# Two gated spectral filters on one core: halves of x added and subtracted in bf16 before the first matmuls, in place of a fold after them

## The chip, the cores and the metric

The kernel runs on one core of a Trainium2 chip. The core has a matrix engine (PE, with its weight loads shown apart as PEld), a vector engine (DVE), a scalar engine (ACT), a general engine (POOL, called GpSimd in code) and a queue engine (SP) that issues nearly all DMA transfers here. Each engine works through its own instruction list strictly in order; an instruction that waits holds up everything behind it in the same list. The metric is the device time of one execution in microseconds (us), lower is better.

## The reference, cut to what matters

For an input x of 2048 rows and 1024 columns, two spectral filters A and B, and a gate vector:

```
g = sigmoid(sum over columns of x * gate_w)           # one number per row
a = irfft2(rfft2(x) * (A_w_r + i A_w_i))              # 2048 x 1024
b = irfft2(rfft2(x) * (B_w_r + i B_w_i))
out = g * a + (1 - g) * b                             # bf16
```

Both filters work on the same x, so the forward transform is made once, the two weighted products and the two inverse transforms share the work, and the row gate is put into the last transform over rows.

## The kernel before, in words

Row index s is split as s = 16*s2 + s1, with s2 (128 values) on the partitions. The columns are brought in by the host as four quarters of 256, the second and fourth reversed, so that symmetric and antisymmetric combinations over the columns are plain sums and differences of quarters. Even output frequencies (parity 0) and odd ones (parity 1) of the column transform are computed separately. Everything runs in three stretches that overlap:

1. **First transform (F1).** For each of 16 s1 values, `f1` (L321) multiplies x by a 128x128 table over s2. For each parity it makes eight matmuls of 128 columns: halves of x are added or subtracted inside PSUM accumulation (second pass with F or -F), which gives two 256-wide parts per parity. The two parts have then to be added and subtracted (the *fold*) to make the two 256-wide inputs of the next step. Two routes exist: `FC` copies one part from PSUM to scratch in `wx` and `FD` folds on DVE (two `tensor_tensor`, one operand from PSUM); `FX` copies both parts and `FP` folds on POOL. The result lies in `y`.
2. **Sixteen units n (0 to 7 parity 0, 8 to 15 parity 1).** For each unit: `F2` (column transform, L450, two half tiles), `T` (copy PSUM to SBUF), `F3` (L480, twiddle and 16-point transform), `X` (copy to SBUF), `P` (L494, product with the weights of both filters, two instructions of 128x2048 for the real and imaginary r), for n below 8 also `Y`, `NA`, `N` (a patch of one column), `J` (`i1`, L537, inverse 16-point transform, two PSUM tiles of 1024), `R` (copy of each tile to SBUF as `rl`), `H` (256 KB stored to a DRAM scratch). The copies are on ACT or DVE as the order list says. Weights W:0 to W:7 land in `Ro`, W:8 to W:11 in `wx`, W:12 to W:15 in `y`.
3. **Second transform and output.** When all eight units of a parity are stored, `L` (L554) loads the scratch back transposed, 512 KB for each pair v of s1 values, into `Re` (parity 0) or `Ro` (parity 1). `V` (`i2`, L565) applies the inverse transform over rows with the gate in its weights `EA` and `EB`; `VC` copies to SBUF; `C` or `U` (L590, L581) applies the inverse column transform: `C` gives two 256-wide parts that still have to be mixed, `U` gives the finished sums at twice the PE columns. Even results end as f32 in `Re` (`E`, or `EX` on ACT or DVE and `EQ` on POOL); the odd ones are added to and subtracted from them (`OR` on DVE straight from PSUM, `OC`+`OP` on POOL, `QD`+`QP` for the two-part form), and `S` stores rows of the output.

The gate: `GH`, `GC`, `GT`, `GK`, `GZ` compute it during stretch 2, `GS` (L434) is the sigmoid on ACT, and `GW` (L439, L440) multiplies it into `EA` and `EB`, four s1 values at a time, on DVE. `tab` (L297) runs a sigmoid on a scratch tile early, so that ACT's table load stands at the start.

What sets the order of the work is `ORDER` (L24 to L68), a list written out: the kernel goes through its tokens one by one, and each appends its instructions to the lists of its engines, under manual scheduling. A token such as `T:3:1:A` reads: copy half 1 of unit 3 on ACT; the last numbers of PE tokens name PSUM banks. So an engine's list is the list's tokens for that engine in the order written, and SP's list holds x, constants, weights, `H`, `L` and `S` in that order too. The `rl` tile has five buffers (`RLB`), `p` three (`PB`).

In the list before, `warm:8 c:A:F1 c:A:gws tab:A` come first (eight matmuls on a zeroed tile, the memset for them on DVE; two constants on ACT's queue; the table). The last units end so: `J:14` and `J:15`, then `H:14:0`, `H:15:1`, `H:15:0`, and behind them on SP `L:0:6`, `L:0:7` and all `L:1`. On PE four `V` and two `C` of parity 0 stand before `J:15`, the other twelve `V` and fourteen `C` between it and the first `V` of parity 1, `V:1:0`.

## Time and profile before

| | |
|---|---|
| runs shown | 117.52, 116.9, 117.24 us; median 117.24 |
| profiled execution | span 115.6 us from the first to the last instruction, granted PE clock 0.985 |
| own time of the profiled execution | not given apart from the span; the median of the runs is 1.64 us above the span |
| PE | 103.6 us busy (90%), 1619 matmuls |
| DVE | 97.0 us (84%), 164 instructions |
| ACT | 84.4 us (73%), 138 instructions |
| POOL | 46.2 us (40%), 74 instructions |
| DMA | 36.79 MB, mean 318 GB/s |

The page gives the span in 40 slices (2.89 us each) with the busy share of each engine in tenths, the chain of work that ended last, and groups of instructions with their mean duration. A matmul's recorded duration contains its pipeline latency, so a busy PE is not PE at its peak: eight 256-column matmuls in a row take 0.109 us each from start to start, while the record of one is 0.273 us. Rates in the text are therefore taken from starts.

### The profile page before, as it was taken

Reading aid. Unit: us, or ns where it says so; the run is one execution under the profiler, and the core shown is the slowest. Engines: PE = TensorE matmul, PEld = TensorE weight load, DVE = VectorE, ACT = ScalarE, POOL = GpSimd, SP = SyncE. Lnnn points to the kernel's source line nnn. Section 1 sums busy time; section 2 is a strip of 40 time slices with the busy share of each in tenths; the row PEclk is TensorE's granted clock in tenths of the full one; section 3 lists DMA queues with packets and bytes.
Section 4 is the critical chain, followed back from the end, with each engine's and each line's share of the span. In section 5 each row is a group of like instructions: output and inputs, shape, how many; then the busy total and the mean of one; then the engine's idle time right before and its main releaser. Section 6 shows DMA issues by size and latency. Waiting matters only on the chain.

```text
span 115.6 us, 3953 instructions
## 1 busy us (share of the span) xinstructions
PE 103.6 (90%) x1619; PEld 71.3 (62%) x1619; DVE 97.0 (84%) x164; ACT 84.4 (73%) x138; POOL 46.2 (40%) x74
## 2 busy tenths in 40 slices
PE   5999999999999699898889899989979999999900
PEld 2499989875567256463445357459859765867400
DVE  0099999999999999999899999999157349999970
ACT  4009488999999999999999999977735844534300
POOL 1066995900000000000000000057986999999920
PEclk9999999999999999999999999999999999999995
DMA  3999999999579999669999999999999992482874
GB/s 90 348 326 401 403 374 367 363 397 408 210 222 324 371 394 373 169 263 397 350 293 354 348 306 401 254 357 382 352 353 411 403 418 98 198 346 119 327 279 181
DMA packets 17794, 36.79 MB, mean 318 GB/s; under 512 B 1904, under 2 KB 10736, under 8 KB 17776
## 3 DMA queue, kind: packets, MB, share of 16 engines
q1 hardware_dynamic: 17488, 36.44, 87.5%
q8 instruction: 12, 0.20, 0.6%
q10 hardware_dynamic: 288, 0.10, 0.4%
q14 instruction: 6, 0.05, 0.1%
HBM read 23.96 MB, written 12.58 MB: 316 GB/s over the span
## 4 chain that ended last, share of the span: by engine, by line
PE 39%; DVE 19%; DMA 16%; ACT 16%; issue 4%; SPq 1%; DVEq 1%; ACTq 0%
ACT rl L204 11%; PE ps L581 9%; PE ps L565 8%; DVE y L382 7%; PE ps L450 6%; PE ps L334 5%; DMA sc<-rl 5%; DMA re<-sc 4%; DMA ig<-cst_ig 4%; PE ps L537 3%; DMA re<-in_x_dram 3%; PE ps L480 3%; DVE p L494 3%; ACT X L204 3%; PE ps L590 3%
## 5 line engine op out<-in xcount | busy, mean ns | idle before, releaser
L615 POOL TENSOR_TENSOR re<-wx 128x256 f32<-128x256 f32 x28 | 19.6, 730 | 55.3 <-DMA re<-sc 53.1
L204 ACT CAST rl<-ps 128x1024 bf16<-128x1024 f32 x29 | 29.6, 1142 | 0.7 <-ACT wx L204 0.7
L204 ACT COPY wx<-ps 128x256 f32<-128x256 f32 (+1 forms) x39 | 17.2, 498 | 10.5 <-PE ps L334 8.2
L537 PE MATMUL ps<-p,wj 32*64 32x512 bf16 x512 | 20.5, 381 | 2.5 <-ACT rl L204 2.0
L204 ACT CAST V<-ps 128x512 bf16<-128x512 f32 x25 | 13.8, 601 | 11.3 <-PE ps L565 8.4
L494 DVE TENSOR_TENSOR p<-X,ro 128x2048 bf16<-128x2048 bf16 x16 | 19.1, 1215 | 0.0
L450 PE MATMUL ps<-fd,y 128*128 128x256 bf16 x128 | 16.5, 273 | 0.4 <-ACT rl L204 0.4
L382 DVE TENSOR_TENSOR y<-ps,wx 128x256 bf16<-128x256 f32 x48 | 16.4, 412 | 0.1
L334 PEld LDWEIGHTS <-re 128*128 128x128 bf16 x256 | 15.2, 100 | 1.6 <-DMA re<-in_x_dram 1.0
L334 PE MATMUL ps<-f,re 128*128 128x128 bf16 x256 | 15.8, 224 | 0.3
L204 ACT CAST T<-ps 128x512 bf16<-128x512 f32 x26 | 15.5, 693 | 0.0
L537 PEld LDWEIGHTS <-wj 32*64 32x64 bf16 x512 | 8.4, 103 | 10.6 <-issue 7.5
L382 POOL TENSOR_TENSOR y<-wx 128x256 bf16<-128x256 f32 x16 | 11.1, 734 | 8.2 <-DVE wx L206 5.9
L635 DVE TENSOR_TENSOR ot<-re,ps 128x512 bf16<-128x512 f32 x22 | 13.8, 681 | 0.4
L450 PEld LDWEIGHTS <-y 128*128 128x128 bf16 x128 | 11.5, 97 | 4.1 <-issue 2.6
L581 PE MATMUL ps<-ig,V 128*128 128x512 bf16 x56 | 13.4, 380 | 0.0
L204 ACT CAST X<-ps 128x1024 bf16<-128x1024 f32 x12 | 13.2, 1118 | 0.0
L206 DVE COPY wx<-ps 128x512 f32<-128x512 f32 (+1 forms) x10 | 5.8, 578 | 7.4 <-PE ps L334 4.8
L480 PE MATMUL ps<-T,wf 64*64 64x256 bf16 (+1 forms) x128 | 10.2, 332 | 1.1 <-DVE np L514 1.0
L590 PE MATMUL ps<-ig,V 128*128 128x256 bf16 x72 | 9.7, 273 | 0.0
L494 DVE TENSOR_TENSOR p<-X,wx 128x2048 bf16<-128x2048 bf16 x8 | 9.4, 1217 | 0.0
L494 DVE TENSOR_TENSOR p<-X,y 128x2048 bf16<-128x2048 bf16 x8 | 9.3, 1215 | 0.0
(60 smaller groups left out, 138.4 us busy)
## 6 DMA issues: line engine op xcount, KB each, us to landing
sc<-rl SPq DMA_DIRECT2D x32, 256.0 KB, 4.7
ro<-in_we_dram SPq DMA_DIRECT2D x8, 512.0 KB, 8.3
re<-sc SPq DMA_DIRECT2D x8, 512.0 KB, 6.1
ro<-sc SPq DMA_DIRECT2D x8, 512.0 KB, 7.7
re<-in_x_dram SPq DMA_DIRECT2D x7, 512.0 KB, 8.0
out_dram<-ot SPq DMA_DIRECT2D x7, 512.0 KB, 2.6
wx<-in_wo_dram SPq DMA_DIRECT2D x4, 512.0 KB, 6.6
y<-in_wo_dram SPq DMA_DIRECT2D x4, 512.0 KB, 5.0
```

What stands on the lines that cost most here:

```text
L204: nc.scalar.copy(out=out, in_=in_)
L334: nc.tensor.matmul(o, lhsT=lh, rhs=rh, start=(h == 0), stop=(h == 1))
L382: Q[e].tensor_tensor(yo[:, v, k:k + n, s1, :], a.rearrange("p (k c) -> p k c", c=4), b.rearrange("p (k c) -> p k c", c=4), op)
L450: nc.tensor.matmul(ps[:, v * 256:v * 256 + 256], lhsT=y[:, v, par, b, 2 * t:2 * t + 2, :, :].rearrange("p j s c -> p (j s c)"), rhs=C["FD" ...
L480: nc.tensor.matmul(view(ps[ho, tt * 512:(tt + 1) * 512], dst), lhsT=lh, rhs=view(T[hp(jh), tt, :], src), start=(w == 0), stop=(w == 1))
L494: nc.vector.tensor_tensor(p[:, r], xb, w, ALU.mult)
L537: nc.tensor.matmul(o, lhsT=lh, rhs=src[r, ri, wi, tt], start=(q == 0), stop=(q == 3))
L565: nc.tensor.matmul(ps[:, ch * 128:ch * 128 + 128], lhsT=RR[par][:, v, ch // 2, s, c0 + 256 * ab:c0 + 256 * ab + 128], rhs=Ew[:, s1, :], st ...
L581: nc.tensor.matmul(ps, lhsT=Vs[par, v][:, s, ch, :], rhs=rh, start=(ch == 0), stop=(ch == 3))
L590: nc.tensor.matmul(ps[:, o:o + 256], lhsT=Vs[par, v][:, s, ch, :], rhs=g[:, o:o + 256], start=(ch % 2 == 0), stop=(ch % 2 == 1))
L615: Q[e].tensor_tensor(EV[:, v, s, 256 * h:256 * h + 256], t[:, 0], t[:, 1], (ALU.add, ALU.subtract)[h])
L635: nc.vector.tensor_tensor(otile(v)[:, s, h, :], EV[:, v, s], PS["O", 1, v, s], (ALU.add, ALU.subtract)[h])
```

## The change

What it does:

- **F1.** A new function `presum` (`PF`) runs on DVE as x arrives: u = lower half + upper half of the columns into `wx`, and the difference in place over the lower half of x, both bf16 in SBUF. It is called once for one s1 twice and then for two s1 at a time. `f1` then makes, for each parity, four matmuls of 256 columns whose table operand is [F, F] or [F, -F], so the fold over the quarters happens in PSUM accumulation. `FE` (`f1e`) copies the finished 512 or 1024 columns to `y`, on ACT or DVE. `FC`, `FD`, `FX` and `FP` are gone, and with them all POOL work of this stretch. `y` is laid out with parity outermost.
- **Products.** `P:n:b` makes both r in one instruction of 128x4096. Weights W:12 to W:15 land in `Ro`, in the places of W:0 to W:3, instead of `y`.
- **Gate weights.** `GW` for s1 0 to 3 and 12 to 15 is on POOL; the other two stay on DVE. `neg` (the negated table for `F3`) is on POOL instead of ACT.
- **Order list.** It is another list from end to end. In front: x:0, x:1, the F1 table on ACT's queue, x:2, `PF:0:1`, and only then `warm:8`, so the memset for the warm matmuls stands on DVE behind the two instructions of `PF:0`. `tab:A` stands close to the end; ACT's list then holds two table loads, one at its start and one in front of the first `GS`. The units run in the order 0, 1, 2, 3, 7, 4, 5, 8, 6, 9, 12, 13, 10, 11, 15, 14. Nine `V` and six `C` of parity 0 stand before `J:14` on PE, and seven `V` and nine `C` between it and the first `V` of parity 1, which is `V:1:5`. All `L:0` stand on SP with eight stores (of units 10 to 15) still behind the last of them; `L:1:5` is the first transfer behind `H:14:1`, the last store. The last stretch has twenty `C` and twelve `U` (before: eighteen and fourteen), 24 `EQ` (28), eight `QD` (four) and eighteen `OR` (22). The mixed rows `QP` are on DVE five times and on POOL three times (before: POOL four times). `EX` copies go to `y` instead of `wx`.

The core of the diff:

```
 ORDER = """
-warm:8 c:A:F1 c:A:gws tab:A x:S:0:1 x:S:1:1 x:S:2:2 x:S:4:2 x:S:6:2 x:S:8:2 x:S:10:2 x:S:12:2 x:S:14:2 c:S:FD:0:1
-F1:1:o:0 F1:1:e:1 FX:1:o:D F1:0:o:2 FC:1:e:D F1:0:e:3 FP:1:o FD:1:e F1:3:o:0 F1:2:e:4 FC:0:e:D F1:3:e:1 gc:P FD:0:e
...
+x:S:0:1 x:S:1:1 c:A:F1 x:S:2:2 PF:0:1 warm:8 PF:1:1 F1:1:0 F1:0:2 x:S:4:2 x:S:6:2 x:S:8:2 x:S:10:2 x:S:12:2 PF:2:2
+F1:3:4 FE:0:A x:S:14:2 c:S:EZ c:S:gws gc:P c:S:w0 PF:4:2 F1:2:6 FE:1:A FE:2:A F1:4:2 F1:5:0 FE:4:A c:S:WJ:0:4
...
-    def f1(s, par, k):
+    def presum(s, n):
+
+        s, n = int(s), int(n)
+        lo, hi = x[:, s:s + n, 0:512], x[:, s:s + n, 512:1024]
+        nc.vector.tensor_tensor(uw[:, s:s + n, :], lo, hi, ALU.add)
+        nc.vector.tensor_tensor(lo, lo, hi, ALU.subtract)
+
+    def f1(s, k, h=""):
+
         s1 = int(s)
...
+        for e in (0, 1) if h == "" else (int(h),):
+            ps = PS["F1", s1, e] = ptile(int(k) + (e if h == "" else 0))
             for b in range(2):
...
+                for pr in range(2):
+                    c = pr * 256 + b * 128
+                    lh = x[:, s1, c:c + 128] if e else uw[:, s1, c:c + 128]
+                    rh = F1[:, 0:2] if pr else bc(F1[:, 0, :]).to_broadcast([P, 2, 128])
+                    o = ps.rearrange("p (v b k) -> p v b k", v=2, b=2)[:, :, b]
+                    nc.tensor.matmul(o, lhsT=lh, rhs=rh, start=(pr == 0), stop=(pr == 1))
+        if h == "":
+            PS["F1", s1] = ptile(k, 2)
+
+    def f1e(s, e, h=""):
 
         s1 = int(s)
...
+        r = slice(0, 256) if h == "" else slice(128 * int(h), 128 * int(h) + 128)
+        src = PS["F1", s1] if h == "" else PS["F1", s1, int(h)]
+        cp(e, yo[:, r, s1, :], src.rearrange("p (k c) -> p k c", c=4))
...
     def prod(n, r):
-        n, r = int(n), int(r)
-        if r == 0:
+        n = int(n)
+        if n not in Ps:
             Ps[n] = wk.tile([P, 2, 2, 4, 256], BF16, name="p", tag="p", bufs=PB)
         X, w, p = Xs[n], Ws[n], Ps[n]
...
+        if r == "b":
+            xb = X[:].rearrange("p r t (a m) -> p r t a m", a=1).to_broadcast([P, 2, 2, 4, 256])
+            wb = w.rearrange("p (r t) a m -> p r t a m", r=1).to_broadcast([P, 2, 2, 4, 256])
+            nc.vector.tensor_tensor(p[:], xb, wb, ALU.mult)
```

## The prediction

> **What bounds the kernel now.** I read the page's slices first, then the engines' instructions in order of time, then the chain that ended last. The slices:
>
> ```profile
> span 115.6 us, 3953 instructions
> ...
> PE   5999999999999699898889899989979999999900
> ...
> DVE  0099999999999999999899999999157349999970
> ACT  4009488999999999999999999977735844534300
> POOL 1066995900000000000000000057986999999920
> ```
>
> Between slices 7 and 26 (20 to 78 us) both DVE and ACT are at nine tenths: the sixteen units are bound by these two together, not by PE. From 80 us ACT and DVE have gaps and PE has none. At the end DVE is full again. The instructions in order of time give the rates (start to start) and the joints:
>
> ```profile
> 1.17 3.60 PE L248 MATMUL ps<-ea 128*128 128x512 bf16 x8 [1.17 <-DVE ea L245]
> 4.87 14.91 PE L334 MATMUL ps<-f,re 128*128 128x128 bf16 x240
> ...
> 24.53 2.35 DVE L494 TENSOR_TENSOR p<-X,ro 128x2048 bf16<-128x2048 bf16 x2
> 71.08 4.62 DVE L494 TENSOR_TENSOR p<-X,y 128x2048 bf16<-128x2048 bf16 x4
> 75.61 0.68 DVE L206 COPY wx<-ps 128x512 f32<-128x512 f32 x1
> 103.12 8.93 DVE L635 TENSOR_TENSOR ot<-re,ps 128x512 bf16<-128x512 f32 x14
> ...
> 47.31 2.97 ACT L204 CAST rl<-ps 128x1024 bf16<-128x1024 f32 x3
> 50.02 1.18 ACT L204 CAST X<-ps 128x1024 bf16<-128x1024 f32 x1
> 77.10 1.01 ACT L204 CAST rl<-ps 128x1024 bf16<-128x1024 f32 x1 [0.71 <-ACT wx L204]
> ...
> 75.96 1.06 PE L537 MATMUL ps<-p,wj 32*64 32x512 bf16 x28 [0.31 <-ACT rl L204]
> 72.74 7.60 SPq L549 DMA_DIRECT2D sc<-rl  x9
> 83.95 4.47 SPq L554 DMA_DIRECT2D ro<-sc  x8
> 89.06 0.99 PEld L565 LDWEIGHTS <-ro 128*128 128x128 bf16 x16
> ```
>
> The reader is to see four joints. F1 starts on PE at 4.87, the first product at 24.53, the last product ends at 75.61 and the last `J` at 77.02. The last store is issued by 80.34, the first `L:1` at 83.95 (SP waits for the stores), the first `V` of parity 1 runs at 89.06. DVE ends at 112.05 and the span 3.55 us later. In the chain of waits
>
> ```profile
> 79.96 0.39 SPq L549
> 80.35 0.05 issue
> 80.40 5.18 DMA re<-sc
> 85.58 0.05 issue
> 85.62 0.62 PE ps L565 x8
> ```
>
> the last store's issue leads to a load, and the load to PE, which then stands without a gap to 108.28. From the last `J` to `V:1:0` PE had 12 `V` (0.45 us each) and 14 `C` (0.44) to do, 11.5 us, so it covered the trip through DRAM but for 0.8 us at 85.6.
>
> Rates: on ACT `T` 0.48, `X` 0.91, `rl` 0.90; on DVE a 512-wide PSUM copy 0.60, a 1024-wide one 1.13, `P` 1.13 (four in 4.53), `OR` 0.64. PE's 256-column matmul 0.109, 128-column 0.058.
>
> **Start and F1.** The warm matmuls run at 0.43 us each, twice the 0.215 us that `U`'s 512 columns take later, and they stand first on PE. Their memset now stands behind `PF:0`, which waits for x:0. Issue at 0.72 plus the shortest landing of these loads, 3.0, gives 3.7. `PF:0` is two two-input SBUF instructions of 512, 0.45 + 0.42 by the `GW` rows (L439, L440), the memset 0.27, the warm block 3.6: PE comes to F1 at 8.5, not 4.87. F1 itself is 128 x 0.109 = 14.0 us instead of 256 x 0.058 = 14.8, and DVE's `presum` (4 x 0.42 + 14 x 0.69, 11 us) follows x as it lands and ends near 17, so it is hidden. `FE` on ACT can start at 8.5 + 1.74 = 10.3; eight of 1024 at 0.95 (between `X`, 0.91, and twice the gate copy with the same short runs, 0.51) and seven of 512 at 0.50 stand before the first `T`: 11.1 us, plus small waits, so 22.0 against 20.45 before. The first product: `F3` waits for the second `T` at 23.0, 0.55 on PE, `X` 0.91: 24.9 against 24.53. The 3.6 us late start thus costs only 0.4 at the first product, because the fold's 16.4 us on DVE and 11.1 on POOL (groups of L382) are gone. Four half `F1` with their copies (1.5 us ACT, 0.6 DVE) are still to come, where before nothing was left.
>
> **The units.** `P` of 4096: 512 elements take 0.424, 2048 take 1.215, so 0.515 ns an element and 0.16 fixed, 2.27 alone, 2.19 in a row; two of 2048 are 2.26. Sixteen save 1.1 us. The other bound is the pace of a one-per-cycle cast (1024 in 1.22), 4.4 each, 35 us more; I take 2.19, since the instruction of before has the same kind of repeated operand. Two pairs of `GW` leave DVE (1.6), `neg` leaves ACT (0.75); ACT gets a table load (1.28, the row at the start).
>
> The page "ScalarE: Activation LUTs" (What ACT_TABLE_LOAD costs) adds a drain of about 1.38 us to the load, which would make this 2.66 and the total 1.4 more; no row here shows the drain.
>
> DVE from the first to the last product: 35.0 + patches 2.4 + eight `T` 4.8 + `FE` 0.6 + `X` 1.13 + five `rl` 5.65 + `GW` 0.8 + 0.1 = 50.5, so 75.4 at no gap (before: 51.1). ACT from its first `T` to the copy `R:14:0` of the last unit: 22 `T` 10.6, 15 `X` 13.6, 25 `rl` 22.5, three `FE` 1.5, gate copy and sigmoids 2.3, table 1.3, nine `VC` and five `EX` that the list puts among them 6.7: 58.5, so 80.5 at no gap. Before, the same count from 25.0 to the end of `R:15:1` (78.11) gives 51.3 in 53.1: 97%. Two full lists that hand work to each other lose that much, so I take 97% again: 82.3. `P:14` waits for `X:14` and then ends at 77.8 (75.4 if DVE alone decided), `J:14` also for `R:15:0` (1.13), which frees its bank, and ends near 80.
>
> **The trip through DRAM.** Behind `R:14:0`: issue of the store 0.4, 3.6 until the first `L:1` (80.34 to 83.95), 4.8 to landing (the shortest of these loads): `V:1:5` at 82.3 + 8.8 = 91.1. PE has seven `V` and nine `C` for that time, 7.1 us, so it is free by 87 and stands some 4 us. This is the step that costs: before, 11.5 us of work lay there. Ends: 80.5 + 0.4 + 2.4 (the shorter store in the chain, 70.30 to 72.64) + 4.8 = 88.1, and 91.1.
>
> **The last stretch.** From `V:1:5`, PE has 16 `V`, 5 `C` and 12 `U` (0.86): 19.7 us (before 20.1 from `V:1:0`). DVE's first `QD` can start after a `V`, a copy and two `C`, 1.8, and it has 8 `QD` (0.62), 5 `QP` (0.6 by the PSUM copies of that size; 0.68 the recorded one) and 18 `OR`: 19.5, so 21.3 at no gap; its last two `OR` need the last `U` at 19.7 plus the waits at its start. I take 22.0, before 23.0 (89.06 to 112.05). POOL has 27 us of `EQ`, `OP`, `QP` (before 32) and no longer decides.
>
> `QP` and two `GW` pairs bring something the trace hardly shows: DVE with two SBUF operands while POOL reads SBUF. One row: POOL's `EQ` at 79.17 starts while DVE's L440 (78.92, 0.42) runs, and takes 0.77 instead of 0.72; L440 is not longer. I take nothing. The other end is one POOL instruction of 0.73 to 1.29 waited for by each of five `QP` and by three products and `GW`, 6 to 10 us; below nothing is excluded, since no engine is sped up by it.
>
> The page "SBUF — State Buffer" (Who interferes with whom) states that such a pair locks the other out for the whole instruction. The row above overlapped by 0.17 us, which speaks against a full lock; by the page I would add half a POOL instruction to each of some eight meetings, about 4 us, an estimate.
>
> **Sum.** 91.1 + 22.0 + 3.55 = 116.65 against 115.6: 1.05 more. The profiled span lies 1.64 below the median of the runs, which I take as what lies around it: 118.3.
>
> **Rivals.**
> - *The trip is covered, faster.* If ACT and DVE keep their lists without gaps and the store lands in 2.4, `V:1:5` is at 88.1 and the time 88.1 + 22.0 + 3.55 + 1.64 = 115.3; with the longer store 116.5. For it: DVE idles only 0.4 us in 24.5 to 75.6. Against: ACT's 97%. It decides when `R:14:0` ends before 81. I put it at 115.9.
> - *POOL and DVE block each other.* Half of the 6 us above, in the stretch where DVE decides: 118.3 + 3 = 121.3. For it: `QP` stands on DVE among 27 us of POOL work. Against: the row at 79.17.
> - *It evens out.* The units are worth what they were, the exchange is 1 us better than taken: 117.2.
> - *The 4096 product loses its pace:* 150 us and more; under 2 in 100, outside the range.
>
> **How the numbers follow.** Forecast (118.3, own range 116.9 to 120) 0.38; covered trip 0.36; blocking 0.12; evens out 0.14. About 0.5% (0.6 us) is what a measurement of this kernel can tell from no change. Faster: the 0.36 and 0.02 of the third; slower: 0.34 of the forecast and the 0.12; same: the rest, 0.04 + 0.12. The range runs from 114.2 (the covered trip with 1 us more in the units, less than a tenth below) to 121.3 (a tenth above).
>
> **What would show it.** Right: F1 on PE near 8.5; first product near 25; DVE and ACT full to about 78 and 82; PE without work for 3 to 5 us right before `V:1:5` at 90 to 92; DVE ending 22 us later; products of 2.27; `GW` on POOL 1.3 each. Wrong: PE busy through that joint, or F1 near 5; products over 3 us; DVE's `QP` well over 0.7 (then the blocking rival). What would overturn the sum is a different efficiency of the two full lists: 3% of 58 us is 1.8 us, more than the whole difference forecast.

## The result, and the profile after

The changed kernel takes 124.25 us (median of 4 runs, 123.63 to 125.33) against 117.24 of the kernel before: the ratio is 1.062, with an interval of 1.054 to 1.069. Slower was right; the size was not: 118.3 us was forecast, with a range up to 121.3. The profiled execution took 125.33 us, the longest of the four, so its segments add up to about 1 us more than the median. Times, ratios and intervals of all versions below leave out runs more than 1.5% above the fastest run of the same version.

The page of the changed kernel: its span, and the span in 40 slices of 3.08 us with busy shares in tenths.

```profile
span 123.2 us, 3610 instructions
...
PE   0399999999999998988698977599992999949900
DVE  0569944799998999899589999975882499999960
ACT  4004999899999998999999959859581863454300
POOL 1000059400000000000607706185989847853980
```

No engine has much more work than before in total (PE 3.0 us less, POOL 0.3, DVE 1.5 and ACT 4.3 more), yet the span is 7.6 us longer: most of the time went into standing. PE is thin at the start, at 58 us (slice 20), from 71 to 80 (slices 24 to 26), at 92 (slice 31), at 108 (slice 36) and at the end.

To say where, each span is cut at five events that every version has: the first product on DVE, the end of the last unit's `J` on PE, the first issue of an `L:1` on SP, the first `V` of parity 1 on PE, and DVE's end. "Predicted" is the sum of the prediction cut at the same events.

| us | to first product | units (to end of last J) | to first L:1 | to first V of parity 1 | last stretch (to DVE's end) | to end of span | span |
|---|---|---|---|---|---|---|---|
| before | 24.5 | 52.5 | 6.9 | 5.1 | 23.0 | 3.55 | 115.6 |
| predicted | 24.9 | 55.1 | 6.3 | 4.8 | 22.0 | 3.55 | 116.65 |
| after | 25.1 | 60.5 | 5.8 | 3.75 | 23.8 | 4.3 | 123.2 |

The last `J`, the first `L:1` and the first `V` of parity 1 after:

```profile
84.51 1.07 PE L499 MATMUL ps<-p,wj 32*64 32x512 bf16 x32
...
91.38 4.00 SPq L516 DMA_DIRECT2D ro<-sc  x8
...
95.13 0.23 PE L527 MATMUL ps<-ea,ro 128*128 128x128 bf16 x1 [2.39 <-DMA ro<-sc]
```

Each version was profiled once, so it matters how far these segments vary by themselves. Four versions have the same list as the changed kernel up to the last `J` (the changed kernel, all `QP` on POOL, and two of the versions of the last stretch): their units take 60.5, 59.4, 60.6 and 61.9 us, the last with PE's clock halved for 3.41 us of them (last section). The first product of the eight versions with this start and no other change before it comes at 24.5 to 26.05. A difference of 1 us in one of these two segments of one trace is therefore not told from no difference.

Against the prediction the profiled execution is 6.55 us longer: +5.4 in the units, +1.8 in the last stretch, +0.7 at the end, +0.2 at the start, and -1.5 in the trip through DRAM.

### The profile page after: what moved, and what is told of

Same layout as the page of the kernel before. It is cut to its first block, busy times and chain, and to the rows that moved or that the text cites. A ratio compares the mean times of both kernels' runs of the same rounds, so it can differ in the third digit from the quotient of the medians.

```text
span 123.2 us, 3610 instructions
## 1 busy us (share of the span) xinstructions
PE 100.6 (82%) x1489; PEld 67.2 (54%) x1491; DVE 98.5 (80%) x119; ACT 88.7 (72%) x129; POOL 46.5 (38%) x59
## 4 chain that ended last, share of the span: by engine, by line
PE 38%; ACT 20%; DVE 16%; DMA 14%; issue 6%; POOL 2%; POOLq 1%; SPq 1%; DVEq 0%; ACTq 0%
ACT y L200 8%; PE ps L527 6%; PE ps L404 6%; DMA re<-sc 5%; PE ps L499 5%; PE ps L437 5%; ACT rl L200 5%; DVE p L453 4%; PE ps L543 4%; PE ps L337 3%; DMA sc<-rl 3%; DMA ro<-sc 3%; DVE ot L607 3%; PE ps L245 3%; DVE rl L202 3%
## 5 line engine op out<-in xcount | busy, mean ns | idle before, releaser
L453 DVE TENSOR_TENSOR p<-X,ro 128x4096 bf16<-128x4096 bf16 x12 | 27.9, 2328 | 0.0
L575 POOL TENSOR_TENSOR re<-y 128x256 f32<-128x256 f32 x24 | 20.2, 870 | 9.5 <-ACT y L200 9.0
L200 ACT CAST y<-ps 128x512 bf16<-128x512 f32 (+1 forms) x18 | 12.6, 808 | 8.4 <-PE ps L337 8.4
L437 PE MATMUL ps<-T,wf 64*64 64x512 bf16 (+1 forms) x128 | 10.6, 333 | 2.0 <-DVE T L202 1.0
L202 DVE CAST rl<-ps 128x1024 bf16<-128x1024 f32 x7 | 8.5, 1220 | 4.1 <-ACT rl L200 1.4
L453 DVE TENSOR_TENSOR p<-X,wx 128x4096 bf16<-128x4096 bf16 x4 | 10.1, 2525 | 0.0
L322 DVE TENSOR_TENSOR wx<-re 128x1024 bf16<-128x1024 bf16 (+1 forms) x9 | 5.6, 623 | 5.4 <-DMA re<-in_x_dram 5.4
L527 PE MATMUL ps<-ea,ro 128*128 128x128 bf16 x64 | 7.9, 219 | 2.4 <-DMA ro<-sc 2.4
L527 PEld LDWEIGHTS <-re 128*128 128x128 bf16 x128 | 7.6, 98 | 3.7 <-DMA re<-sc 1.9
L527 PE MATMUL ps<-ea,re 128*128 128x128 bf16 x64 | 8.3, 220 | 1.6 <-DMA re<-sc 1.6
```

Of the source, the lines that this page charges most:

```text
L200: nc.scalar.copy(out=out, in_=in_)
L202: Q[e].tensor_copy(out=out, in_=in_)
L322: nc.vector.tensor_tensor(uw[:, s:s + n, :], lo, hi, ALU.add)
L437: nc.tensor.matmul(view(ps[ho, tt * 512:(tt + 1) * 512], dst), lhsT=lh, rhs=view(T[hp(jh), tt, :], src), start=(w == 0), stop=(w == 1))
L453: nc.vector.tensor_tensor(p[:], xb, wb, ALU.mult)
L527: nc.tensor.matmul(ps[:, ch * 128:ch * 128 + 128], lhsT=RR[par][:, v, ch // 2, s, c0 + 256 * ab:c0 + 256 * ab + 128], rhs=Ew[:, s1, :], st ...
```

## What the profile of the changed kernel shows, place by place

**DVE and POOL shut each other out.** The timeline of DVE, then that of POOL, in the second half of the units (start, duration, engine, line, operation, output and input, count, idle time before and its releaser):

```profile
65.90 3.24 DVE L453 TENSOR_TENSOR p<-X,wx 128x4096 bf16<-128x4096 bf16 x1
69.06 1.37 DVE L391 TENSOR_TENSOR ea<-ea,e 128x512 bf16<-128x512 bf16 x1
...
73.14 2.28 DVE L453 TENSOR_TENSOR p<-X,wx 128x4096 bf16<-128x4096 bf16 x1
75.34 2.82 DVE L453 TENSOR_TENSOR p<-X,ro 128x4096 bf16<-128x4096 bf16 x1
```

```profile
59.42 1.15 POOL L391 TENSOR_TENSOR ea<-ea,e 128x512 bf16<-128x512 bf16 x1 [36.45 <-ACT ea L386]
...
65.47 1.52 POOL L391 TENSOR_TENSOR ea<-ea,e 128x512 bf16<-128x512 bf16 x1 [3.67 <-ACT ea L386]
67.07 3.08 POOL L392 TENSOR_TENSOR eb<-e,ea 128x512 bf16<-128x512 bf16 x1
73.79 2.22 POOL L575 TENSOR_TENSOR re<-y 128x256 f32<-128x256 f32 x1 [3.63 <-ACT y L200]
```

A product is 2.28 us alone, `GW` on POOL 1.15 (row at 59.42), `EQ` 0.73 alone. The product that starts at 65.90 is recorded at 3.24, because POOL's `GW` has the memory until some 66.9 (65.47 + 1.52, less the 0.1 us by which records overlap); POOL's next instruction, issued at 67.07, then ends only at 70.15, 1.0 after the product is through (its record is 3.08). The `GW` half at 69.06 on DVE takes 1.37 instead of 0.42. At 73.79 the same happens with `EQ`: 2.22 instead of 0.73, and it makes the product at 75.34 wait in turn: 2.82. DVE loses 0.96 + 0.95 + 0.54 = 2.45 us in this stretch, and from 62.43 to the end of the last product (81.49) it is never idle for more than 0.04 us, so the last product is late by all of it.

**A load stands behind a store, and PE behind the load.** SP's queue, and the PE instruction that waits:

```profile
72.65 0.37 SPq L511 DMA_DIRECT2D sc<-rl  x1
73.07 1.88 SPq L516 DMA_DIRECT2D re<-sc  x2
```

```profile
80.19 0.23 PE L527 MATMUL ps<-ea,re 128*128 128x128 bf16 x1 [1.62 <-DMA re<-sc]
81.19 1.07 PE L499 MATMUL ps<-p,wj 32*64 32x512 bf16 x32
```

The second of the two loads issued from 73.07 on is `L:0:1` (issued at 73.58, landed at 80.15). It stands on SP behind `L:0:2` and `H:13:0`, the store at 72.65, which waits for a copy that DVE finishes at 72.63; of that copy's lateness, 0.96 + 0.95 us are the two meetings before it. `V:0:1` on PE waits for that load until 80.19, and behind it in PE's list stands `J:15` (81.19), whose product was done at 78.16. The last `J` follows at 84.51, 3.0 us after its own product, so in this trace it is PE's list that sets it; the first `L:1` issues at 91.38 and `V:1:5` runs at 95.13.

**The last stretch.** DVE, then POOL:

```profile
97.19 2.48 DVE L602 TENSOR_TENSOR pq<-re,ps 128x512 f32<-128x512 f32 x4 [4.00 <-PE ps L552]
...
102.41 3.50 DVE L607 TENSOR_TENSOR ot<-pq 128x512 bf16<-128x512 f32 x3
...
107.62 2.36 DVE L607 TENSOR_TENSOR ot<-pq 128x512 bf16<-128x512 f32 x2
109.90 9.05 DVE L595 TENSOR_TENSOR ot<-re,ps 128x512 bf16<-128x512 f32 x15
```

```profile
104.22 1.13 POOL L575 TENSOR_TENSOR re<-y 128x256 f32<-128x256 f32 x1
105.31 1.72 POOL L607 TENSOR_TENSOR ot<-pq 128x512 bf16<-128x512 f32 x1
...
112.84 2.50 POOL L591 TENSOR_TENSOR ot<-re,wx 128x512 bf16<-128x512 f32 x2 [3.42 <-DMA out_dram<-ot]
```

From 97.19 to 118.95 DVE is never idle for more than 0.22 us. Five `QP` (L607) take 5.86 us, 1.17 each, where the prediction put 0.6; POOL's instructions beside them grow too (1.72 for `QP`, 1.13 for `EQ`; 1.27 and 0.73 alone). POOL then stands 3.42 us for an output buffer, because the first store on SP is that of v = 5, which waits for DVE's last `QP` and issues at 110.05 (before: 98.51). So POOL ends at 119.71, after DVE, and the last store with it: 4.3 instead of 3.55 behind DVE's end. The stores on SP, before and after:

```profile
98.51 13.90 SPq L652 DMA_DIRECT2D out_dram<-ot  x9
```

```profile
110.05 10.02 SPq L612 DMA_DIRECT2D out_dram<-ot  x9
```

## The experiments

Diffs name tokens of the order list; all start from the changed kernel unless said otherwise.

**GW back on DVE.**

```
-... GW:P:0 ... GW:P:12 ...
+... GW:D:0 ... GW:D:12 ...
```

> The changed kernel with both GpSimd gate-weight pairs back on DVE (nothing else). Exclusion theory (a DVE instruction with two SBUF operands and a POOL instruction wait for each other to the end): the product of 3.24 us at 65.90 and the DVE gate weight of 1.37 us at 69.06 go back to 2.28 and 0.42, the POOL pair of 1.52 and 3.08 is gone; DVE gains 1.9 of waits and pays 4 x 0.40 = 1.6, so the time moves by -1 to +0.5 us from 124.25. Rival (GpSimd is free help, the long rows are something else): DVE only pays, +1.6 us, and a product over 3 us stays.

123.62 and 125.41 us, 1.061 [1.051, 1.072]. No gain, as the theory of an exclusive lock had it: what DVE no longer waits (1.9) it now works (1.7). The rows say the same: the product and the `GW` pair in the places of the long rows above are back at their own lengths, which the rival excluded.

```profile
66.69 2.28 DVE L452 TENSOR_TENSOR p<-X,wx 128x4096 bf16<-128x4096 bf16 x1
68.89 0.42 DVE L390 TENSOR_TENSOR ea<-ea,e 128x512 bf16<-128x512 bf16 x1
69.35 0.42 DVE L391 TENSOR_TENSOR eb<-e,ea 128x512 bf16<-128x512 bf16 x1
```

The units take 61.7 us in the trace, but PE's clock is 0.50 in them from 81.29 to 84.70, while PE works off its list before the last `J`; the version with that half clock and `GW` on POOL has 61.9. So the trace shows neither gain nor loss of the edit in the units.

**The loads up.** `L:0:1`, `L:0:7` and `L:0:2` right behind `L:0:6`.

```
-L:0:6 H:12:1 L:0:4 ... L:0:3 L:0:7 ... H:13:0 ... L:0:2 ... L:0:1 ...
+L:0:6 L:0:1 L:0:7 L:0:2 H:12:1 L:0:4 ... L:0:3 ... H:13:0 ...
```

> The changed kernel with the loads L:0:1, L:0:7 and L:0:2 right behind L:0:6 on SP, in front of the stores of units 12 and 13. Queue theory (V:0:1 waits until 80.19 for a load that stands behind a store on SP, and J:15 stands behind V:0:1 on PE): V:0:1 no longer waits, J:15 starts by 78.5 instead of 81.26, the last J ends 2 to 3 us sooner, time -2 to -3 us, 121.5 to 122. Rival (the two full lists of DVE and ACT set the last J anyway): the wait moves to the next item, time within 0.6 us of 124.25.

123.13 and 123.94 us. PE's wait at 80 is gone, the units take 58.4 us (-2.1; in the other versions that have the load in its old place that wait is 1.0 to 2.1 us) and the first `L:1` issues at 88.64. The end moved by 1.1 only: the last stretch became 25.4 us. The reason is in the windows of PE at its standstill (us; busy us of PE, PEld, DVE, ACT, POOL with counts; then the granted clock, DMA share, GB/s):

```profile
90.21:93.62 3.41, 1.20 (x20) 1.11 (x20) 0.52 (x1) 0.69 (x2) 3.41 (x6) 1.00 0.94 375
93.62:97.03 3.41, 3.41 (x25) 2.77 (x23) 1.70 (x3) 1.83 (x5) 1.95 (x3) 0.50 1.03 420
97.03:100.44 3.41, 3.41 (x55) 3.32 (x54) 2.48 (x5) 2.18 (x5) 1.27 (x1) 1.00 1.02 407
```

PE stood 2.21 us for the first `L:1`, and the granted clock then was 0.50 for 3.41 us: 1.7 us of PE's work lost, against 1.55 us by which the stretch is longer than in the changed kernel's profile, where the clock stayed at 1.00.

**All QP on POOL.**

```
-QP:3:0:1:D QP:5:1:1:D QP:3:1:1:D ... QP:5:0:0:D QP:5:0:1:D
+QP:3:0:1:P QP:5:1:1:P QP:3:1:1:P ... QP:5:0:0:P QP:5:0:1:P
```

> The changed kernel with all eight QP on POOL instead of three. Exclusion theory: DVE loses five instructions of 1.14 (5.7 us) from its last stretch, POOL gains five but its own go from 1.7 to 1.8 back to 1.28; DVE ends 3 to 5 us sooner, POOL then ends last, time -1.5 to -3 us. Rival (POOL was already the last engine, at 119.7, so more work there lengthens it): +1 to +3 us.

124.81 and 125.82 us, 1.068 [1.060, 1.076]. The theory's gain of 1.5 to 3 us is not there; the middle, 1.1 us more than the changed kernel, is at the low end of what the rival said, and the interval overlaps the changed kernel's. In the trace POOL becomes what the stores wait for (first one at 111.93), and DVE stands 6.0 us for PE; but that execution took 127.69 us and has PE's clock at 0.50 for two times 3.41 us in the last stretch, so how much of it is POOL's is not shown.

**Warm matmuls and table load in front.**

```
-x:S:0:1 x:S:1:1 c:A:F1 x:S:2:2 PF:0:1 warm:8 PF:1:1 ... V:1:0:1:6 tab:A U:1:2:1:3
+warm:8 x:S:0:1 x:S:1:1 c:A:F1 tab:A x:S:2:2 PF:0:1 PF:1:1 ... V:1:0:1:6 U:1:2:1:3
```

> The changed kernel with the warm matmuls first in the list and the table token right behind the F1 table, as in the kernel before. F1 on PE starts at 5.0 to 5.8 instead of 8.73, ACT's list loses 1.28 us at 57. Theory that ACT and DVE carry the start through the units: the first product comes 2 to 3 us sooner, the table another 1.3, time -3 to -4.5 us, 120 to 121. Rival (the late start is hidden, as the prediction had it, and only the table counts): -0.5 to -1.5 us.

121.6 and 122.39 us, 1.040 [1.033, 1.047]. `F1` starts at 4.96 instead of 8.5, the first product at 22.8: 1.7 us earlier than in the kernel before. The first `L:1` issues 4.2 us earlier, the span is 2.7 shorter; the granted clock behind PE's 2.44 us standstill was 0.50 for 3.41 us here too, and the last stretch took 25.4. The two edits were not tried apart; in the changed kernel PE stood 1.28 us for the activation behind the table load at 57, and here it does not.

**GW and loads together.** Both diffs above.

> The changed kernel with two edits together: both GW pairs back from POOL to DVE (alone they changed nothing), and L:0:1, L:0:7, L:0:2 right behind L:0:6 on SP (alone the first L:1 issued 2.7 us earlier). Theory 'two causes, one behind the other': while V:0:1 holds PE until 80 the DVE locks lie hidden, and the other way round; together the first L:1 issues 3.5 to 5 us earlier than the changed kernel's 91.4, so at 86.4 to 87.9, and the last product ends at 78 to 79.5. Rival 'the two full lists simply lose more than 3%': the first L:1 stays where the loads alone put it, at 88 to 89, and the last product ends near 81. For the end both say little: with the last stretch bound by its own order (first store near 109), 122.5 to 124.5 us by either.

122.42 us (122.07 to 122.43), 1.040 [1.036, 1.044]. As the events stand, the first `L:1` (89.53) and the end of the last product (81.19) are near the rival's figures (88 to 89, near 81), not the theory's 3.5 to 5 us. But the profiled execution took 124.65 us and has its first product only at 26.05; counted from there the units take 57.4 us, 1.0 less than with the loads alone. That is within what two traces of one list differ by, so for the locks' price on the path it shows no more than "about 1 us or nothing"; the times, about 1 us below those with the loads alone, point to the former. The last stretch has the clock at 0.50 for 3.41 us too and takes 25.2.

**The last stretch without QP, two versions.**

```
-C:1:5:1:0 QD:5:1:1 ... QP:5:1:0:P ... C:1:3:1:4 QD:3:1:1 ... S:S:5 ... S:S:3
+U:1:5:1:0 OR:5:1:1 ... U:1:3:1:4 OR:3:1:1 ...
-E:5:1:A E:5:0:D ... E:3:1:A E:3:0:A
+EX:5:1:y:A EQ:5:1:0:P EQ:5:1:1:P EX:5:0:y:D ... EX:3:0:y:A EQ:3:0:0:P EQ:3:0:1:P
```

> The changed kernel with the odd rows of v = 5 and v = 3 made as the others are: U in place of C (four times), OR in place of QD (eight), no QP, the even parts through EX and EQ on POOL, and each store right behind its last OR. Theory 'the last stretch is DVE's list, made longer by QP at 1.17 instead of 0.6': from V:1:5 DVE has 26 OR of 0.61, so 15.9 us instead of 21.8, and PE (19.7 and four times 0.4) decides with about 21.5; the first output store issues near 101 to 103 instead of 110.05, POOL's 3.4 us wait on the stores is gone, and the span ends 2 to 3 us earlier: 121.3 to 122.5 us. Rival 'POOL is the bound of this stretch': eight more EQ (5.8) against three QP (4.8) delay the EQ that OR waits for, DVE stands waiting for POOL, and the time stays at 124 us or above. Rival 'the output's 4 MB set the end': first store earlier, end the same.

> The changed kernel with the warm matmuls and the table load at the front, the three loads L:0:1, L:0:7, L:0:2 up, and v = 5 and 3 in the last stretch as in e6_tail. Theory 'three separate losses, start, joint and last stretch, that add once the last stretch follows': 4 us at the first L:1 from the start, 1.5 to 2.7 more from the loads, 2 to 3 from the last stretch: first L:1 at 84.5 to 86.5, 116 to 119 us. Rival 'they overlap, and something further stands behind': 119.5 to 121.5 us, with DVE or PE idle for over 3 us in the last stretch.

132.35 us (1.127 [1.122, 1.132]) and 125.75 (1.069 [1.066, 1.072]): both misses. In both, the copies of v = 5 and 3 go into slots whose content had still to be added, so some even rows are sums of other data; the instructions are those described. What spoilt the test is my own edit: with the stores right behind the last `OR` of v = 5 and 3, SP holds later `L:1` behind them (the fourth load issues at 102.08 in the first version), and the seventeen `EQ` that POOL has from 94.6 to 107.0 hold DVE for 4.13 us. They say only that loads must not stand behind stores here, and that POOL's list is near full.

**v = 5 alone, and its store behind the last load.**

```
-E:5:1:A EQ:4:1:1:P E:5:0:D ... C:1:5:1:0 QD:5:1:1 ... QP:5:1:0:P ... S:S:5 (after the last QP)
+EX:5:1:w:A EQ:4:1:1:P EX:5:0:w:D EQ:5:1:0:P EQ:5:1:1:P EQ:5:0:0:P EQ:5:0:1:P ... U:1:5:1:0 OR:5:1:1 ... L:1:0 S:S:5
```

> The changed kernel with the odd rows of v = 5 alone made as most others are: U in place of C, four OR in place of four QD and four QP, the even parts through EX into the space of W:8 to W:11 and four EQ on POOL ahead of those that stand there; the store of v = 5 behind the last load on SP. Theory 'QP beside POOL at 1.17 makes the last stretch DVE's': DVE has 3.5 us less to do, first output store at 102 to 106 instead of 110, the span 1.5 to 2.5 us shorter: 121.5 to 123 us. Rival 'POOL is the next bound': OR waits for the EQ of v = 5 or 2, DVE stands over 2 us in the last stretch, 123.8 us or more.

124.81 us (124.46 to 125.28), 1.060 [1.053, 1.068]: no gain. The time is the rival's, but not for its reason. The first store went to 102.80, POOL's wait for a buffer is gone and the end is 3.58 behind DVE again. But the stretch took 24.0 us: the clock was 0.50 from 95.99 to 99.40, right behind PE's 2.37 us standstill, DVE stood 6.0 us before its first `OR`, and from 95.9 to 117.4 the chain of work that ended last runs on PE alone, matmul behind matmul. With PE's clock at 1.00 the same stretch takes 22.4 us (everything together, below).

**The price of QP and of a meeting.** Instructions on scratch data: `ZQ` has QP's form (on DVE), `ZP` EQ's (on POOL).

```
+P:3:b ZQ ZQ ... P:4:b ZQ ZP ZP ZP ZP ZQ ZQ ZQ ...
...
+        nc.vector.tensor_tensor(zb(512).rearrange("p (s d) -> p s d", s=2), t[:, :, 0], t[:, :, 1], ALU.add)
...
+        nc.gpsimd.tensor_tensor(zb(1408).bitcast(F32), zb(512).bitcast(F32), zv()[:, 0, 0], ALU.add)
```

> The changed kernel with instructions of QP's form (two f32 operands of 128x512 from SBUF, bf16 out) added on DVE on a scratch tile, two where POOL does nothing (behind the product of unit 3) and four beside four added f32 additions of 128x256 on POOL (behind the product of unit 4). Price 'QP costs 1.1 us by itself, because of its operands': the first two take 1.1 to 1.2 each, as long as the recorded 1.14 to 1.17. Price 'QP costs 0.6 to 0.7 and the rest is POOL's lock': the first two 0.6 to 0.7, those beside POOL 1.1 to 1.4. In both the four beside POOL show what the meeting costs on each side: by a full lock each of POOL's 0.73 grows by up to one DVE instruction. The time itself is some 6 to 9 us longer and says nothing.

```
+P:4:b ZQ:a (fourteen ZP) ZQ:b ZQ:b ZQ:b ZQ:b ...   (ZQ:b and ZP write to places that no other of them reads)
```

> The changed kernel with fourteen added f32 additions of 128x256 on POOL (the form of EQ, 0.73 us alone) started in the quiet stretch, and beside them on DVE four added instructions of QP's form (0.70 recorded, 0.61 from start to start when alone), then the patches, copies from PSUM and products that stand there anyway. Theory 'a DVE instruction with two SBUF operands and a POOL instruction shut each other out for their whole length': the four of QP's form take 1.1 to 1.4 us from start to start, the additions beside them likewise; a product met by POOL is recorded at 2.3 to 3.0 and the addition that meets it at up to 3.0; copies from PSUM stay at 0.69 and 1.22 and POOL's additions beside them at 0.73. Rival 'they share the bandwidth': all of them grow in proportion, products to 3 and more, copies from PSUM too. The time itself says nothing.

DVE in the first of the two (L626 is QP's form):

```profile
37.09 1.41 DVE L626 TENSOR_TENSOR eb<-ea 128x512 bf16<-128x512 f32 x2
...
45.20 0.69 DVE L626 TENSOR_TENSOR eb<-ea 128x512 bf16<-128x512 f32 x1
```

DVE in the second (L482 is the patch, with both operands in SBUF), then one of POOL's additions in it:

```profile
43.34 1.29 DVE L626 TENSOR_TENSOR eb<-ea 128x512 bf16<-128x512 f32 x2
44.66 3.36 DVE L626 TENSOR_TENSOR eb<-ea 128x512 bf16<-128x512 f32 x3
...
48.04 0.64 DVE L482 TENSOR_TENSOR p<-np 128x16 bf16<-128x16 f32 x1
48.56 0.68 DVE L202 CAST T<-ps 128x512 bf16<-128x512 f32 x1
...
55.60 2.28 DVE L453 TENSOR_TENSOR p<-X,ro 128x4096 bf16<-128x4096 bf16 x1
57.91 0.64 DVE L482 TENSOR_TENSOR p<-np 128x16 bf16<-128x16 f32 x1
```

```profile
55.75 2.72 POOL L629 TENSOR_TENSOR eb<-eb,ea 128x256 f32<-128x256 f32 x1
```

In the first, a wait I had made between the two groups kept them from meeting; it shows the price alone: 0.69 to 0.71. In the second they meet. The first two of the five start before POOL's first addition can stop them and are 0.61 apart; the other three start 1.13 apart and take 1.09 to 1.10 each, as expected (1.1 to 1.4), and POOL's additions beside them 1.05 instead of 0.73. The patch goes from 0.23 to between 0.64 and 0.75 for 16 elements: it waits for a POOL instruction. Copies from PSUM stay at 0.68. Where the product comes first (55.60) it keeps its 2.28, and POOL's addition, issued 0.15 us later, is recorded at 2.72; where POOL comes first the product is at 2.40 to 2.81. Sharing in proportion (the rival) is excluded by the unchanged copies and by the product at 2.28 with an addition waiting beside it.

The page "SBUF — State Buffer" of the Trainium skill (Who interferes with whom) says this outright: a DVE instruction with two SBUF inputs and a GpSimd instruction that reads SBUF exclude each other, for the whole instruction. The rows above agree with it: the one that comes second waits.

**The new arithmetic in the order of before.** `PF`, `f1` and `FE` in place of `FC`, `FD`, `FX`, `FP`, on the engines of `FC` and `FX`; the rest of the list as before.

```
-F1:1:o:0 F1:1:e:1 FX:1:o:D F1:0:o:2 FC:1:e:D F1:0:e:3 FP:1:o FD:1:e
+PF:1:1 F1:1:0:1 F1:1:1:0 FE:1:D:1 PF:0:1 F1:0:2:1 FE:1:D:0 F1:0:3:0
```

> The arithmetic of the changed kernel in the order list of before: halves added and subtracted on DVE, fold inside the first matmuls, FE in place of FC and FX on the same engines, FD and FP gone, y and W:12 to W:15 as in the changed kernel, but products of 2048, GW, neg, the table load, the units' order, the loads and the last stretch as before. Theory 'the loss is the list's, not the arithmetic's': the start is no later than before (first T at 21 to 23), first L:1 at 81 to 85, last stretch as before: 114.5 to 117.5 us. Rival 'the halves on DVE themselves put the start back': first T at 24 or later, 118.5 to 121 us.

124.56 us, 1.056 [1.048, 1.064]: a miss. The units take 52.7 us, as before to 0.2 us, and the last stretch 22.9; all of the loss is the start, with the first product at 32.1. Neither theory nor rival had that. DVE's waits say where: 9.6 us for the first `X` of ACT. `FE` copies 512 columns (0.49 us in a row) where `FC` copied 256 (0.35), and `FD`'s share on DVE is gone while ACT got more; ACT also has its first copy only at 13.15 (before: 8.88), behind PE. The arithmetic moves work from DVE to ACT, and an order written for the other split pays for it; the shares of the two were not separated.

**Wide products in the kernel before.**

```
-P:1:0 ... P:1:1
+P:1:b
```

> The kernel before with one change: each product as one instruction of 128x4096 in place of two of 128x2048, at the place of the first of the two. Theory 'the wide product is worth nothing either way': 116.7 to 117.8 us, products 2.27 to 2.29 against two of 1.17 or so. Rival 'a list with wide products holds up what stood between the halves': DVE's N, T and X copies come 1.1 us later, PE waits for them, 118 to 120 us.

118.79 us (nine runs), 1.013 [1.008, 1.017]: slower by a little over 1%, within the rival's 118 to 120. A product of 4096 is 2.28 against two of 1.22 recorded (2.35 for two), so DVE gains 0.07; PE's waits for the patch's first half, which stands behind a product on DVE, go from 1.0 to 2.1 us, and the units from 52.5 to 53.7.

**The grafted list.** The changed kernel's list, with warm matmuls and table in front, up to the first product; behind it the list of before with its 2048-wide products; in the second version the first weights in the order of its products.

```
-F1:1:o:0 F1:1:e:1 FX:1:o:D ... W:S:3 ... F2:2:1:5 ... (before, up to the first product)
+warm:8 x:S:0:1 x:S:1:1 c:A:F1 tab:A x:S:2:2 PF:0:1 ... X:0:A (changed, units 0 and 1 exchanged)
 P:1:0 ... (before, from here on)
```

> The arithmetic of the changed kernel (halves on DVE, fold inside the first matmuls, FE, its y, W:12 to W:15 in Ro) with the changed list's own first part up to the first product, warm matmuls and table load in front; behind it the list of before, with its 2048-wide products, units, loads and last stretch. Theory 'the units' new order costs the time, the arithmetic does not': first product at 22.5 to 23.5 (before 24.5), from there to the end of the last J 52.5 to 53.5 as before (52.5), first L:1 at 82 to 84 (before 83.95): 114.3 to 117 us. Rival 'the arithmetic itself costs': the copies FE crowd ACT and DVE where FC and FD did not, the units take over 55 us: 118 us or more.

> g1_graft with the first six weights loaded in the order of the products (W:1, W:0, W:2, W:3, W:7, W:10). Theory 'the arithmetic is worth nothing either way': first product at 23.5 to 24.5, units 53 to 53.5, 116.8 to 118 us, within 0.6% of before. Rival 'the earlier start is kept': first product under 23.3 and 115.5 to 116.6 us. Rival 'the copies FE cost': first product early but units 54 or more, 118 us or more.

118.83 us, 1.011 [1.007, 1.015], and 119.16, 1.016 [1.011, 1.022]: the theories miss in both; in the second the figures are those of its second rival. In the first the first product waits 1.39 us for its weights and comes at 25.2; the units take 53.25. In the second it comes at 23.6, and the units take 54.7: what is gained in front is lost behind. Four `FE` that were put off stand there, three on ACT and one on DVE, and DVE waits 1.5 us for its own; that they are the whole of it was not tried. In this order the new arithmetic brings nothing; it costs 1 to 2%.

**The trip through DRAM covered.** The loads up, and `J:14` with its copies ahead of three `V` and two `C`.

```
-C:0:1:1:3 ... GW:D:8 V:0:2:0:5 ... V:0:7:1:6 ... C:0:1:0:7 ... J:14:0:2 R:14:1:D ... R:14:0:A
+J:14:0:2 R:14:1:D R:14:0:A C:0:1:1:7 ... GW:D:8 V:0:2:0:5 ... V:0:7:1:6 ... C:0:1:0:7
```

> The changed kernel with L:0:1, L:0:7, L:0:2 behind L:0:6 as in e2_loads_up, and J:14 with its two copies right behind R:15:0, ahead of three V and two C that stood before it. Theory 'the trip is uncovered because PE's parity-0 work stands in front of the last J': from the first product to the end of J:14 56 to 57 us (58.4 with the loads alone), the first L:1 near 86 to 87, PE's wait right before V:1:5 under 0.5 us instead of 2.2 to 2.4; of these 2 us about half arrive at the end: 122.5 to 124 us. Rival 'J:14 waits for its product anyway': no more than 0.5 us earlier than with the loads alone, wait before V:1:5 still 2 us or more.

122.43 us (121.84 to 123.33), 1.043 [1.038, 1.048]; the profiled execution took 124.61 us, and its events are counted from its first product. PE no longer stands before `V:1:5` and the clock stays at 1.00. But `J:14` waits 1.09 us for a copy that frees its bank, so the units take 59.3 (58.4 with the loads alone): the time from the first product to `V:1:5` is 68.9 us against 68.0. Filling PE's standstill did not bring `V:1:5` forward. The times are about 1 us below those of the loads alone all the same; the half clock, which this trace does not have, would be worth about that, but it was not tried alone. Theory and rival hold in part: the cover works, J comes no earlier.

**Everything together.** Warm matmuls and table in front, `GW` on DVE, loads up, `J:14` ahead, v = 5 through `U` and `OR`; in the second version `EX:0:0` also ahead of `R:15:1`.

> The changed kernel with warm matmuls and table load in front, GW on DVE, the three loads up, J:14 ahead of the five PE steps, and v = 5 in the last stretch through U and OR. Theory 'five losses that add in part': first product 22.8, last J ends 55 to 56 us later, first L:1 at 83.5 to 85, from there 31.5 to 33 to the end: span 115.5 to 118, time 117 to 119.5 us, at or just above before. Rival 'behind them stands a bound of the new order itself, PE and DVE both full in the last stretch': 120 us or more, though the first L:1 comes as early as said.

> g3_all with two copies on ACT exchanged: EX:0:0, which frees the bank that J:14 waits for (1.09 us in g3_all), ahead of R:15:1. Theory 'PE is what bounds this version from the units on, and this wait is the last on it': J:14 0.8 to 1.1 us earlier, all of it kept to the end since PE then stands nowhere: 116 to 116.9 us, 0.5 to 1% below before. Rival 'J:14 then waits for the copy of R:15:0 on DVE, and DVE and POOL hold the last stretch': 117 to 117.6 us.

117.35 us (ten runs), 0.998 [0.994, 1.001], and 117.09 (ten runs), 0.999 [0.995, 1.003]: the time of the kernel before, and 6.9 us less than the changed kernel. The arithmetic, the products and the order of the units are those of the changed kernel. Span, PE and PEclk (granted clock in tenths) of the first of them:

```profile
span 115.6 us, 3604 instructions
...
PE   5999999899999987998999897968899999999910
...
PEclk9999999999999999999999999999999999999995
```

PE has at least eight tenths in all but four slices up to slice 38; the lowest behind the first, with six, is slice 27 (75 to 78 us), where `J:14` begins a wait of 1.09 us. No version is measurably faster than the kernel before. The second edit brought nothing that can be measured (0.5 to 1% was expected): J's wait moved on to the product (0.58) and to the copy on DVE (0.73), as the rival said.

The segments of these runs, cut at the same events:

| us | to first product | units | to first L:1 | to first V | last stretch | to end | span | PE's clock at 0.50 for 3.41 us in |
|---|---|---|---|---|---|---|---|---|
| after | 25.1 | 60.5 | 5.8 | 3.75 | 23.8 | 4.3 | 123.2 | - |
| GW on DVE | 25.2 | 61.75 | 5.8 | 3.8 | 22.7 | 4.3 | 123.6 | units |
| loads up | 24.5 | 58.4 | 5.7 | 3.85 | 25.4 | 4.3 | 122.2 | last stretch |
| warm and table in front | 22.8 | 58.5 | 5.9 | 3.7 | 25.4 | 4.3 | 120.6 | last stretch |
| GW and loads | 26.05 | 57.4 | 6.1 | 3.8 | 25.2 | 4.3 | 122.9 | last stretch |
| v = 5 through U | 25.8 | 60.6 | 5.7 | 3.9 | 24.0 | 3.6 | 123.5 | last stretch |
| loads up, J:14 ahead | 25.8 | 59.3 | 4.2 | 5.5 | 23.8 | 4.3 | 122.8 | - |
| everything | 23.5 | 56.5 | 5.2 | 4.5 | 22.4 | 3.6 | 115.6 | - |

Alone, the edits move the time by little: `GW` +0.3 us, v = 5 through `U` +0.6, the loads -0.7, the start -2.2 (middle of the runs against 124.25; the first two are no difference by their intervals). The loads with `GW` or with `J:14` ahead bring 1.8 each, everything 6.9. Each edit takes away one of several waits that lie side by side or behind one another, and in the traces of the four single versions a half clock of PE eats some of the gain. Which edit has which share of the 6.9 us was not tried: there is no version with all but one.

## Why the prediction was right and wrong

**1. Start: right.** `F1` at 8.53 (8.5 said), first `T` 22.01 (22.0), first product 25.09 (24.9). What it did not say is that this start throws something away: with the warm matmuls and the table load in front the same arithmetic has its first product at 22.8.

**2. Units: the step that failed, +5.4 us.** The prices were right: product 2.28, `GW` on POOL 1.15 (1.3 said), table load 1.28. The count of DVE was right at no gap (50.5), and the idle time added to it (2.4) nearly so (3.1). Missing were two terms.
- The locks, "I take nothing": 2.45 us on DVE. The row that misled was the `EQ` of before at 79.17, which began 0.17 us before a DVE instruction of 0.42 ended. So short a meeting, between records that overlap by 0.1 us anyway, cannot tell a lock from none. `P:14` ended at 81.49 instead of 77.8. The two rows of before, POOL's and DVE's:

```profile
79.17 0.77 POOL L615 TENSOR_TENSOR re<-wx 128x256 f32<-128x256 f32 x1 [0.60 <-ACT wx L204]
```

```profile
78.92 0.42 DVE L440 TENSOR_TENSOR eb<-e,ea 128x512 bf16<-128x512 bf16 x1
79.27 0.68 DVE L206 COPY wx<-ps 128x512 f32<-128x512 f32 x1
```

- A wait through SP: `V:0:1` on PE behind `L:0:1`, behind `H:13:0`, behind a DVE copy. I priced PE's list by its sum and did not follow the place of each load on SP. `J:14` ended 4.1 us after the last product, not 2.2. This is the wait that set the last `J` in the profile; moving three loads took it away and gave 2.1 us of the units. What the locks are worth behind it is less sure: about 1 us or nothing.

The 97% taken for ACT did not hold: ACT stood for PE (1.75 us for the `V` that waited for its load, 1.2 for an `X`), and `R:14:0` ended at 86.74 instead of 82.3.

**3. Trip through DRAM: length right, its weight overrated.** From `R:14:0` to `V:1:5` 8.4 us (8.8 said); PE stood 2.4 us there (4 said), because it was late itself. "The step that costs" it was not by its own length: with the gap filled and J no earlier, `V:1:5` came no earlier. What such a gap did cost, in the versions above though not in the changed kernel's own profile, is the granted clock behind it, about 1.5 us, which I had not priced at all.

**4. Last stretch: +1.8, and +0.7 at the end.** `QP` on DVE at 0.6 was the wrong term: 1.17 beside POOL, 5 x 0.57 = 2.9 us, of which 1.8 are left after smaller gains. Alone it costs 0.69, so the price was right and the cover wrong. The end came later because POOL stood 3.42 us for an output buffer: I had taken the store order for harmless. In the version with all edits, which has only four `QP` left, the two terms are 22.4 and 3.6, close to the 22.0 and 3.55 of the prediction.

**5. The rivals.** "POOL and DVE block each other" was the right mechanism and the one with the worst odds of the three that counted (0.12): 121.3 us was its price. The queue wait, which no rival had, came on top. "The trip is covered" and "it evens out" were wrong. "The 4096 product loses its pace" was wrong: 2.28.

**6. The page on SBUF against the row.** Its estimate (4 us more) would have put the time at 122.3; I preferred one row with a meeting of 0.17 us. Where a row is that short and a page that definite, the row should have been kept as the other end of the range, with its weight.

## What to carry to other kernels

Before an instruction with two SBUF operands is put on DVE, or anything on POOL, look at what the other engine does in that stretch: here each meeting made one of the two wait for up to the whole of the other (0.95 us on DVE, 1.9 on POOL), and copies from PSUM lost nothing. Price a list not by its sum alone: follow each late load and store through its queue to the engine behind it. And when single repairs bring little, the waits may lie side by side; only the run with all of them mended told that the list, not the arithmetic, held the 6.9 us. Before a segment of one trace is read as the worth of an edit, look at the granted clock in it and at how far two traces of the same list differ.

## What the runs showed of the hardware that was not expected

**A standstill of PE of some 2 us can halve its clock for 3.41 us or longer; it depends on where it falls.** In all traces of this case the recorded granted clock is either 1.00 or 0.50, and it changes only at steps of 3.41 us (or a multiple: with the loads up it is 1.00 for 25 such periods, 0.50 for one, 1.00 for seven; behind four longer standstills, of 3.65 to 5.1 us, in the versions without `QP` and those with scratch data, it is 0.50 for two). The changed kernel cut at its own steps, around PE's standstill of 2.39 us from 92.74 to 95.13, with columns as in the windows above:

```profile
91.22:94.63 3.41, 1.52 (x18) 1.16 (x16) 1.84 (x3) 1.62 (x4) 3.41 (x6) 1.00 0.59 185
94.63:98.05 3.42, 2.92 (x40) 2.56 (x41) 0.86 (x2) 2.06 (x4) 3.40 (x5) 1.00 1.03 420
```

Here the standstill falls on two periods, with 1.89 us (3.41 - 1.52) in the first, and the clock stays at 1.00. With the loads up a shorter one, 2.21 us, falls into one period (90.21 to 93.62 above), and the next period is at 0.50. So it is in all traces, cut at their own steps: the twelve periods at full clock in which PE was idle for 2.07 us or more are each followed by one at 0.50. Of those with less, one is (1.85 us), two are not (1.97 and 1.89), and none with 1.7 or less is. The price can be read from the last stretch: with the same list but for `tab:A` it takes 25.4, 25.4 and 25.2 us with a half clock in it, and 22.7 (`GW` on DVE), 23.8 and 23.8 without.

The page "TensorE: Matmul & The Clock Gate" of the Trainium skill (Part 1) describes such a gate, with half the clock after an idle window of about 3.4 us, and windows that run freely. Half the clock and the length of the window agree with the traces; but about 2 us of idle time in a window were enough here. That the standstill is the cause was not tried by itself: what speaks for it is that every half clock in these traces, up to PE's last instruction, begins right behind a period with at least 1.85 us of idle time.

**The table load in the middle of a list cost its own length.** ACT's timeline of the changed kernel:

```profile
55.93 1.06 ACT L200 CAST X<-ps 128x1024 bf16<-128x1024 f32 x1
57.02 1.28 ACT L386 ACT_TABLE_LOAD   x1
58.31 1.03 ACT L386 ACTIVATE ea<-ps 128x1024 bf16<-128x1024 f32 x1
```

The load begins 0.02 us behind the instruction before it, and the activation follows 0.01 us behind the load. The drain of 1.38 us that the prediction quoted beside it does not show.
